# Moving one tile's load and its crossbar transfer ahead of a larger load, at the start of a fused attention and MLP kernel

## The chip, the cores and the metric

The kernel runs on one core of a Trainium2 chip. The metric is the time of one execution on the device, in microseconds (us). Each experiment is compared with the kernel before in interleaved rounds on one chip.

## The reference, cut to what matters

The input `x` has 2048 rows (tokens) of 640 numbers in bf16. One branch is a linear attention with 32 heads, the other a shift mixer with an MLP; a sigmoid gate mixes the two.

```python
qkv = x @ wqkv                       # -> q, k, v, 32 heads of 20
pq, pk = phi(q), phi(k)              # phi(t) = (t + 1 if t > 0 else exp(t)) + 1e-6
kv  = einsum("bhsd,bhse->bhde", pk, v)
o   = einsum("bhqd,bhde->bhqe", pq, kv) / den
a   = o.reshape(B, S, D) @ wo
# [...] b = MLP branch of x;  g = sigmoid(sum(x * gate_w))
return g * a + (1 - g) * b
```

This is about the first 20 us: `x @ wq` and `x @ wk` for the first tiles of 128 tokens each (tiles 0, 1, 2, ...).

## The kernel before

In this kernel TensorE (PE) reads `x` transposed (`xT`, features on the partitions) in both products. Tiles 0, 1 and 2 are transposed by PE itself. From tile 3 on, the SP queue issues a DMA for each tile that transposes `x_tok` (tokens on the partitions) into `xT` (`DMA_TRANSPOSE` in the traces); I call it a crossbar transfer. I call the transfer of tile t "Tt" (T3, T4, ...), and the load of tiles 4 to 7, one DMA of 640 KB, "XC1".

This is the order in which SP issues things in the kernel before:

```python
dma_in(x_tok[:, 0, :], x2[0:128, :], "x0")
dma_in(x_tok[:, 1, :], x2[128:256, :], "x1")
load_wq(0)
dma_in(x_tok[:, 2, :], x2[256:384, :], "x2")
for k in range(1, KD):                      # KD = 5 slices of the query weights
    load_wq(k)
for k in range(KD):                         # 5 slices of the key weights
    dma_in(wkg[:, k, 0:D], A_wqkv[128 * k:128 * (k + 1), D:2 * D], "wk%d" % k)
    if k == 2:
        dma_in(x_tok[:, 3, :], x2[384:512, :], "x3")
# [...]
for c in range(1, NCH):                     # c = 1 is XC1
    dma_in(x_tok[:, 4 * c:4 * c + 4, :], x2[512 * c:512 * (c + 1), :].rearrange("(n p) d -> p n d", p=128), "xc%d" % c)
    for t in range(3 if c == 1 else 4 * c, 4 * c + 4):
        sch.dma("sp", xT[:, :, 128 * t:128 * (t + 1)], x_tok[:, t, :], "trx%d" % (t % 4), transpose=True)
```

SP issues in this order in the traces. A transfer first waits for the load of its tile, and everything behind it on SP waits with it: tile 3's load landed at 9.84 us and T3 was issued at 9.85, XC1 landed at 13.52 and T4 was issued at 13.54, and SP issued nothing else while it waited. PE keeps the program's order too (first products of tiles 3, 4, 5 and 6 at 14.81, 17.53, 21.07 and 24.06 us). It goes through the first tiles like this:

```python
addA(("warm",), 0.0, lambda: warmup(WARM, 0.834))   # products on constants while the loads come
# [...] transposes of tiles 0, 1
addA(("q", 2), 4.08, q_three)                       # q of tiles 0, 1, 2 as the slices land
addA(("k", 1), 2.72, k_two)                         # k of tiles 0, 1
addA(("k", 2), 1.36, lambda: k_tile(2))
for i in range(3, NT + 2):
    # [...]
    addA(("q", i), 1.36, lambda t=i: q_tile(t))     # first use of tile i's xT: waits for Ti
    addA(("k", i), 1.36, lambda t=i: k_tile(t))
    # [...]
```

## Time and profile before

| | before |
|---|---|
| time, first 3 executions | 260.52 us median (260.36 to 261.09) |
| span of the profiled execution | 259.8 us |
| PE busy | 254.8 us (98%) |
| XC1: issued, landed | 7.41, 13.52 us |
| T3: issued, landed; PE starts on tile 3 | 9.85, 14.27; 14.75 us |
| T4: issued, landed; PE starts on tile 4 | 13.54, 17.45; 17.50 us |

"PE starts" is here, and in what follows, the first weight load of the tile's products.

Three lines of the page: the busy time of each engine, then the chain of work that ended last, by engine and by line of the kernel.

```profile
...
PE 254.8 (98%) x1655; PEld 133.0 (51%) x1686; DVE 152.0 (59%) x288; ACT 106.5 (41%) x216; POOL 93.6 (36%) x152
...
PE 98%; issue 1%; DVE 0%; POOL 0%; POOLq 0%
PE ps L600 61%; PE ps L1160 21%; PE ps L790 8%; PE ps L882 2%; PE ps L855 1%; PE ps L1072 1%; PE ps L1142 1%; PE ps L883 1%; PE ps L611 1%; DVE x_tok L639 0%; PE ps L962 0%; PE ps L991 0%; PE ps L1139 0%; POOL xn L659 0%; POOLq L1306 0%
...
```

PE is busy 98% of the span and makes up 98% of the chain: at each step back from the last instruction, what the work had waited for was other work of PE. (Some matmul records are missing from this trace: 1655 of 1686 are there. So the busy times of two traces are not to be subtracted.)

The list of PE's waits over the whole execution (line, what was waited for, us in total, times, longest):

```profile
...
PE ps L855 <- POOL xn L659: 1.1, 1, 1.1
PE ps L600 <- issue: 0.2, 1, 0.2
PE ps L1160 <- issue: 0.2, 1, 0.2
```

The only wait over 0.2 us is the one at the start.

The SP queue, from about 4 to 24 us (start, length, line; L285 is a plain load, L281 a crossbar transfer). The five transfers of 9.85 are merged into one line; between them SP waits for XC1.

```profile
...
4.08 0.43 SPq L285 DMA_DIRECT2D wq<-in_A_wqkv_dram  x1
4.56 1.38 SPq L285 DMA_DIRECT2D wkg<-in_A_wqkv_dram  x3
5.98 0.43 SPq L285 DMA_DIRECT2D x_tok<-in_A_x_dram  x1
6.46 0.91 SPq L285 DMA_DIRECT2D wkg<-in_A_wqkv_dram  x2
7.41 0.43 SPq L285 DMA_DIRECT2D x_tok<-in_A_x_dram  x1
9.85 9.57 SPq L281 DMA_TRANSPOSE xT<-x_tok  x5
19.47 0.58 SPq L285 DMA_DIRECT2D x_tok<-in_A_x_dram  x1
23.88 1.21 SPq L281 DMA_TRANSPOSE xT<-x_tok  x1
```

The issue of T4, and how long it takes to land; then PE's weight loads, whose times show when PE goes from one tile to the next (`wkg` is a key product of tile 3, the `wq` after it the first product of tile 4):

```profile
...
L281 SPq DMA_TRANSPOSE xT<-x_tok x1: 1207/1207/1207, 13.5 to 13.5; - x1
...
DMA to landing us min/median/max: 3.9/3.9/3.9
```

```profile
...
16.11 1.40 PEld L600 LDWEIGHTS ps<-wkg,xT 128*128 128x128 bf16 x10
17.50 1.38 PEld L600 LDWEIGHTS ps<-wq,xT 128*128 128x128 bf16 x10
```

T4 is issued at 13.54 and takes 3.92 us, so it lands at 17.45, and PE starts on tile 4 at 17.50. There is no idle time in brackets on that line. PE came to tile 4 just when the tile came.

### The profile page before, as it was taken

The numbers are of one execution on the slowest core, as the hardware profiler recorded it, in microseconds if no ns is written. First come the engines' busy times: TensorE is split into PE (matmuls) and PEld (weight loads), VectorE is DVE, ScalarE is ACT, GpSimd is POOL, SyncE is SP. The second block draws the span as 40 slices with busy tenths as digits, with TensorE's granted clock in tenths as the row PEclk, the third lists the DMA queues.
The fourth block names the chain that finished last, engine by engine and source line by source line (L and its number), as shares of the span: only waits on it lengthen the run. The fifth ranks groups of instructions, "written<-read, shape, count | busy, mean of one in ns | idle before, by whom it ended". The sixth has DMA issues, their size and how long they took to land.

```text
span 259.8 us, 4263 instructions
## 1 busy us (share of the span) xinstructions
PE 254.8 (98%) x1655; PEld 133.0 (51%) x1686; DVE 152.0 (59%) x288; ACT 106.5 (41%) x216; POOL 93.6 (36%) x152
## 2 busy tenths in 40 slices
PE   8999999999999999999999999999999999999996
PEld 4555555554445455555444545554455544455453
DVE  1487787899912799999998407993033410143233
ACT  1396767751355766685854140005500045200000
POOL 4003996869963019667904202230011110021001
DMA  6955886581756991552726650132000020000211
GB/s 185 288 86 150 175 207 154 166 140 39 110 113 124 360 327 32 76 101 52 104 46 122 124 73 0 39 83 82 0 3 0 3 101 0 0 3 1 103 50 50
DMA packets 51390, 25.16 MB, mean 97 GB/s; under 512 B 42750, under 2 KB 49959, under 8 KB 51370
## 3 DMA queue, kind: packets, MB, share of 16 engines
q1 hardware_dynamic: 49984, 21.47, 36.0%
q0 software_dynamic: 1136, 3.28, 5.1%
q8 instruction: 13, 0.21, 0.4%
q10 hardware_dynamic: 250, 0.14, 0.2%
q14 instruction: 7, 0.06, 0.1%
HBM read 12.05 MB, written 2.62 MB: 56 GB/s over the span
## 4 chain that ended last, share of the span: by engine, by line
PE 98%; issue 1%; DVE 0%; POOL 0%; POOLq 0%
PE ps L600 61%; PE ps L1160 21%; PE ps L790 8%; PE ps L882 2%; PE ps L855 1%; PE ps L1072 1%; PE ps L1142 1%; PE ps L883 1%; PE ps L611 1%; DVE x_tok L639 0%; PE ps L962 0%; PE ps L991 0%; PE ps L1139 0%; POOL xn L659 0%; POOLq L1306 0%
## 5 line engine op out<-in xcount | busy, mean ns | idle before, releaser
L600 PE MATMUL ps<-xnT,w 128*128 128x512 bf16 x348 | 80.4, 379 | 0.7 <-issue 0.2
L1160 PE MATMUL ps<-w,h2T 128*128 128x512 bf16 (+1 forms) x409 | 58.3, 298 | 0.5 <-issue 0.2
L656 ACT ACTIVATE h2T<-ps 128x512 bf16<-128x512 f32 x52 | 30.5, 598 | 67.6 <-PE ps L600 67.5
L600 PEld LDWEIGHTS ps<-xnT,w 128*128 128x128 bf16 x360 | 34.2, 98 | 38.5 <-issue 0.9
L639 DVE SCALAR_TENSOR_TENSOR x_tok<-ps,stg,abx 128x512 bf16<-128x512 f32 (+1 forms) x32 | 17.3, 550 | 61.5 <-PE ps L1160 61.5
L622 POOL TENSOR_SCALAR abx<-x_tok,stg 128x640 f32<-128x640 bf16 x16 | 15.3, 956 | 99.1 <-DVE x_tok L639 94.9
L1160 PEld LDWEIGHTS ps<-w,h2T 128*128 128x128 bf16 x416 | 32.1, 98 | 24.9 <-issue 1.1
L622 POOL TENSOR_SCALAR xn<-x_tok,st 128x640 bf16<-128x640 bf16 x32 | 34.9, 1099 | 13.8 <-DMA xnT<-xn 13.3
L656 ACT ACTIVATE Er<-ps 128x640 bf16<-128x640 f32 x32 | 22.4, 708 | 17.7 <-PE ps L600 7.9
L655 ACT ACTIVATE junk<-x_tok 128x640 bf16<-128x640 bf16 x32 | 23.7, 739 | 3.1 <-DVE x_tok L637 2.6
L656 ACT ACTIVATE hsT<-ps 128x512 bf16<-128x512 f32 (+1 forms) x32 | 18.9, 593 | 13.1 <-PE ps L600 12.7
L600 PE MATMUL ps<-M_sb,pqnT 128*128 128x128 bf16 (+1 forms) x156 | 23.6, 297 | 0.3
L600 PE MATMUL ps<-w,hsT 128*128 128x512 bf16 (+1 forms) x160 | 23.7, 299 | 0.0
L639 DVE SCALAR_TENSOR_TENSOR abx<-ps,stg,abx 128x640 f32<-128x640 f32 x16 | 14.1, 883 | 12.6 <-PE ps L600 11.6
L600 PE MATMUL ps<-wkg,xT 128*128 128x130 bf16 (+1 forms) x138 | 21.1, 298 | 0.1
L600 PE MATMUL ps<-wq,xT 128*128 128x128 bf16 (+1 forms) x128 | 19.7, 298 | 0.1
L600 PEld LDWEIGHTS ps<-w,hsT 128*128 128x128 bf16 x160 | 13.3, 98 | 12.1
L600 PEld LDWEIGHTS ps<-M_sb,pqnT 128*128 128x128 bf16 x160 | 13.2, 98 | 10.8
L790 PE MATMUL ps<-pk_tok,x_tok 128*128 128x512 bf16 x79 | 17.7, 379 | 0.1
L622 DVE TENSOR_SCALAR Er<-Er 128x640 bf16<-128x640 bf16 x32 | 11.6, 361 | 9.6 <-ACT Er L656 9.3
L1101 DVE TENSOR_TENSOR pq_tok<-pq_tok,dnr 128x300 bf16<-128x300 bf16 (+1 forms) x48 | 16.8, 403 | 0.6
L637 DVE SCALAR_TENSOR_TENSOR x_tok<-ps,x_tok 128x640 bf16<-128x640 f32 x16 | 13.1, 820 | 6.5 <-PE ps L600 5.9
(79 smaller groups left out, 229.1 us busy)
## 6 DMA issues: line engine op xcount, KB each, us to landing
w<-in_B_w_dram SPq DMA_DIRECT2D x1, 2160.0 KB, 9.7
w<-in_B_w_dram SPq DMA_DIRECT2D x1, 2080.0 KB, 15.2
x_tok<-in_A_x_dram SPq DMA_DIRECT2D x3, 640.0 KB, 5.5
out_dram<-x_tok SPq DMA_DIRECT2D x3, 640.0 KB, 3.1
w<-in_B_w_dram POOLq DMA_DIRECT2D x8, 160.0 KB, 3.7
wq<-in_A_wqkv_dram SPq DMA_DIRECT2D x5, 160.0 KB, 3.2
wkg<-in_A_wqkv_dram SPq DMA_DIRECT2D x5, 160.0 KB, 3.9
wv<-in_A_wqkv_dram POOLq DMA_DIRECT2D x1, 800.0 KB, 5.5
```

Of the source, the lines that this page charges most:

```text
L600: ins = e.matmul(out_ap, l, r, start=(i == 0), stop=(i == n - 1))
L611: ins = e.transpose(o, s_, ident[:])
L622: return engf(lambda e: e.tensor_scalar(out_ap, in_ap, s1, s2, op0, op1), rd, [out_ap], cost=cost)
L637: return dve(lambda e: e.scalar_tensor_tensor(out_ap, in0, scalar, in1, op0, op1, accum_out=accum), rd, [out_ap, accum], cost=cost + 70.0)
L639: return dve(lambda e: e.scalar_tensor_tensor(out_ap, in0, scalar, in1, op0, op1), rd, [out_ap], cost=cost)
L655: return act(lambda e: e.activation(out_ap, in_ap, func, bias=bias, scale=scale, accum_out=accum), rd, wr, cost=cost)
L656: return act(lambda e: e.activation(out_ap, in_ap, func, bias=bias, scale=scale), rd, wr, cost=cost)
L790: ins = e.matmul(o, l, r, start=(t0 + q_ == 0), stop=(t0 + q_ == NT - 1))
L855: ins = e.matmul(ps[:, b, 0:n], xn[:, 0, 0:128], xn[:, 0, 0:128].unsqueeze(1).to_broadcast([128, n // 128, 128]), start=True, stop=True)
L882: e.matmul(ps[:, b, 0:512], l, w[:, k, 0:512], start=(k == 0), stop=(k == KD - 1))
L1101: dve(lambda e, o=o, i0=i0, i1=i1: e.tensor_tensor(o, i0, i1, ALU.mult), [i0, dnr[:, 1, sd, :]], [o], cost=cost)
L1160: ins = e.matmul(o, l, r, start=False, stop=(i == KFF - 1), skip_group_check=(n0 > 0))
```

## The change

The intent is to have tile 3 earlier: its load goes behind the first key slice, and its transfer no longer stands behind the issue of XC1.

```diff
     for k in range(KD):
         dma_in(wkg[:, k, 0:D], ...)
-        if k == 2:
+        if k == 0:
             dma_in(x_tok[:, 3, :], x2[384:512, :], "x3")
+
+    def x_turn(t):
+        sch.dma("sp", xT[:, :, 128 * t:128 * (t + 1)], x_tok[:, t, :], "trx%d" % (t % 4), transpose=True)
+
+    x_turn(3)
     # [...]
     for c in range(1, NCH):
         dma_in(x_tok[:, 4 * c:4 * c + 4, :], ...)
-        for t in range(3 if c == 1 else 4 * c, 4 * c + 4):
-            sch.dma("sp", xT[:, :, 128 * t:128 * (t + 1)], x_tok[:, t, :], "trx%d" % (t % 4), transpose=True)
+        for t in range(4 * c, 4 * c + 4):
+            x_turn(t)
```

The instructions of PE, DVE, ACT and POOL and their waits are the same in both kernels; only the order on SP differs. (The line numbers of PE's groups behind the edit are 5 higher in the changed kernel.)

## The prediction

> **What bounds the kernel now.** TensorE. The page gives PE 254.8 of 259.8 us busy (98%), the chain of waits is 98% PE, and in the list of waits PE's only wait over 0.2 us is the 1.1 us at its start. Almost nothing is left to win: the change helps only where PE waits for a moved transfer, and hurts where it makes one late.
>
> **What the change does.** PE, DVE, ACT and POOL keep their order and waits; only the SP queue changes. Nothing is added or removed.
> 1. The load of x tile 3 moves from behind the third key slice to behind the first. Slices 1 and 2 move back one place.
> 2. Transfer T3 (crossbar transpose of tile 3) goes ahead of the load of tiles 4-7 (XC1). SP issues in order, so XC1 now waits behind T3's wait for tile 3 and T3's issue.
>
> **Costs, from the trace of before** (issues in the timeline, landings in the semaphore records). 128x640 loads land about 0.45 us apart (8.53, 8.97, 9.42, 9.84 for slices 0, 1, 2 and tile 3). XC1 was issued at 7.41 and landed at 13.5 (6.1 us). T3 was issued at 9.87 (SP held 1.3 us) and landed at 14.3. PE first uses tile 3 at 14.81, tile 4 at 17.50, tile 5 at 21.07, tile 6 at 24.06.
>
> After:
> - Tile 3 lands at about 8.97, slices 1 and 2 at 9.42 and 9.84; PE wants those at 10.97 and 11.25. No wait.
> - T3 is issued at about 9.0 and lands at 11.5 to 12.5. PE wants it at 14.81: 2 us earlier buys nothing.
> - XC1 is issued at about 10.3, 2.9 us later. Without T3 inside its stream it should take what the load of tiles 8-11 takes, also issued right behind a transfer: 4.4 us. It lands at about 14.7, 1.2 us later.
> - T4 waits for XC1. In before it was issued at 13.5; its last semaphore came at 17.46 and PE began on tile 4 at 17.50: no slack. [...] After, T4 is issued at about 14.75, where T5 was in before, and T5 landed at 17.95. So T4 lands at about 18.0, and PE waits about 0.5 us before tile 4.
> - T5-T7 and the loads of tiles 8-15 are about 1.2 us later: T5 at 19.3 against 21.07, T7 at about 22 against 27.05, T8 at about 27.5 against 30.04. No wait.
>
> **On the critical path:** a loss of about 0.5 us, once, and no gain. PE has no later idle time to absorb it.
>
> **Predicted time:** 261.0 us, 260.3 to 262.0 in 8 of 10. Faster by over 2%: 0.01; within 2%: 0.97; slower by over 2%: 0.02.
>
> **What would show it.** SP timeline: T3 at about 9.0, XC1 at about 10.3, T4 at about 14.7. T3 lands over 2 us before PE uses it. A new PE gap of 0.2 to 1 us before the first product of tile 4 at about 17.5, and none elsewhere. Everything later shifted by as much.
>
> **What would make it wrong.** If XC1, free of T3's interleaved packets, takes 3.5 us, T4 lands by 17.4 and nothing changes. If the stall of copies right behind a transfer (the load of tiles 8-11 lost about 1 us of its 4.4 so) is longer here[...], T4 lands after 18.5 and the loss is over 1 us. The spread of before's three runs is 0.7 us, so 0.5 us is near what they resolve.

An issue at about 14.75 and the 3.16 us that T5 took in before put T4's landing at about 18.0, 0.5 us after 17.50. The stall that the last paragraph names is in the trace of before: T7 landed at 20.66 us, and the load of tiles 8 to 11, issued at 19.47, moved at about 61 GB/s from 20.5 to 21.0 us and 49 from 21.0 to 21.5, against 394 from 22.0 to 22.5.

## The result, and the profile after

| | before | after |
|---|---|---|
| time, 6 executions each (the first 3 of before are those above) | 260.88 us median (260.36 to 261.12) | 260.93 us median (260.71 to 261.25) |
| ratio | | 1.0006, 95% interval 0.9992 to 1.0019 |
| XC1: issued, took, landed | 7.41, 6.11, 13.52 | 10.06, 4.38, 14.44 |
| T3: issued, took, landed | 9.85, 4.41, 14.27 | 8.71, 2.87, 11.58 |
| PE starts on tile 3 | 14.75 | 14.35 |
| T4: issued, took, landed | 13.54, 3.92, 17.45 | 14.45, 2.96, 17.41 |
| PE starts on tile 4 | 17.50 | 17.46 |

A ratio is the mean time of one kernel's fast executions over that of the other's of the same rounds, so it is not quite the ratio of the medians quoted beside it.

There is no difference that these executions resolve. But the chain has moved. The same three lines of the page:

```profile
...
PE 256.4 (99%) x1686; PEld 132.8 (51%) x1686; DVE 152.5 (59%) x288; ACT 106.6 (41%) x216; POOL 94.2 (36%) x152
...
PE 92%; DMA 4%; SPq 2%; DVE 0%; issue 0%
PE ps L600 60%; PE ps L1165 22%; PE ps L795 8%; DMA x_tok<-in_A_x_dram 3%; SPq L285 1%; DMA xT<-x_tok 1%; PE ps L1077 1%; PE ps L1147 1%; SPq L281 0%; DVE x_tok L639 0%; PE ps L967 0%; PE ps L996 0%; PE ps L1144 0%
...
```

PE's share of the chain fell from 98% to 92%, and the loads and transfers of `x` have come in with 4% and SP's issues with 2%. The list of PE's waits says the same: it has one that was not there before.

```profile
...
PE ps L860 <- POOL xn L659: 1.1, 1, 1.1
PE ps L600 <- DMA xT<-x_tok: 0.2, 1, 0.2
```

The SP queue, as above. T3 now stands alone at 8.71 and XC1 behind it at 10.06:

```profile
...
4.07 0.44 SPq L285 DMA_DIRECT2D wq<-in_A_wqkv_dram  x1
4.56 0.43 SPq L285 DMA_DIRECT2D wkg<-in_A_wqkv_dram  x1
5.03 0.43 SPq L285 DMA_DIRECT2D x_tok<-in_A_x_dram  x1
5.51 1.85 SPq L285 DMA_DIRECT2D wkg<-in_A_wqkv_dram  x4
8.71 1.30 SPq L281 DMA_TRANSPOSE xT<-x_tok  x1
10.06 0.57 SPq L285 DMA_DIRECT2D x_tok<-in_A_x_dram  x1
14.45 5.77 SPq L281 DMA_TRANSPOSE xT<-x_tok  x4
20.26 0.58 SPq L285 DMA_DIRECT2D x_tok<-in_A_x_dram  x1
```

T4, and PE's weight loads around the start of tile 4 (the first of the two lines is cut by the window; the brackets give the idle time of the weight loader and what ended it):

```profile
...
L281 SPq DMA_TRANSPOSE xT<-x_tok x1: 1806/1806/1806, 14.5 to 14.5; - x1
...
DMA to landing us min/median/max: 3.0/3.0/3.0
```

```profile
...
15.98 1.13 PEld L600 LDWEIGHTS ps<-wkg,xT 128*128 128x128 bf16 x8
17.46 1.36 PEld L600 LDWEIGHTS ps<-wq,xT 128*128 128x128 bf16 x10 [0.34 <-DMA xT<-x_tok]
...
```

And the part of the chain of waits from 5 to 20 us, in order of time (start, us, what). In before the same stretch of the chain is nothing but PE.

```profile
...
5.03 3.66 DMA x_tok<-in_A_x_dram
8.70 0.02 issue
8.71 1.30 SPq L281
10.01 0.05 issue
10.06 4.38 DMA x_tok<-in_A_x_dram
14.44 0.02 issue
14.45 2.96 DMA xT<-x_tok
17.41 0.05 issue
17.46 2.61 PE ps L600 x15
```

Read it downwards: tile 3's load, T3's issue, XC1, T4, and then PE on tile 4. This is the path that the prediction named. It was longer than PE's own work by about 0.34 us, the idle time of the weight loader, not by 0.5 us. (The 0.2 us in the list of waits is too small, because the ends of matmuls are modelled. From PE's start on tile 3 to its start on tile 5 it took 6.60 us here and 6.26 us in the first profile of before and in others without a wait: 0.34 us more.) And yet PE starts on tile 4 at the same time in the two profiles, 17.50 and 17.46. Two things have to be explained: why T4 did not land later than before, and why PE waited for it only in the changed kernel.

### The profile page after: what moved, and what is told of

It reads as the page before. It is cut to its first block, busy times and chain, and to the rows that moved or that the text cites. A ratio compares the mean times of both kernels' runs of the same rounds, so it can differ in the third digit from the quotient of the medians.

```text
span 259.7 us, 4294 instructions
## 1 busy us (share of the span) xinstructions
PE 256.4 (99%) x1686; PEld 132.8 (51%) x1686; DVE 152.5 (59%) x288; ACT 106.6 (41%) x216; POOL 94.2 (36%) x152
## 4 chain that ended last, share of the span: by engine, by line
PE 92%; DMA 4%; SPq 2%; DVE 0%; issue 0%
PE ps L600 60%; PE ps L1165 22%; PE ps L795 8%; DMA x_tok<-in_A_x_dram 3%; SPq L285 1%; DMA xT<-x_tok 1%; PE ps L1077 1%; PE ps L1147 1%; SPq L281 0%; DVE x_tok L639 0%; PE ps L967 0%; PE ps L996 0%; PE ps L1144 0%
## 5 line engine op out<-in xcount | busy, mean ns | idle before, releaser
L600 PE MATMUL ps<-xnT,w 128*128 128x512 bf16 x360 | 81.5, 379 | 0.0
L600 PE MATMUL ps<-M_sb,pqnT 128*128 128x512 bf16 (+1 forms) x160 | 24.3, 299 | 0.0
L600 PE MATMUL ps<-wq,xT 128*128 128x512 bf16 (+1 forms) x130 | 19.8, 299 | 0.2 <-DMA xT<-x_tok 0.2
L622 DVE TENSOR_SCALAR Er<-Er 128x640 bf16<-128x640 bf16 x32 | 11.6, 362 | 9.8 <-ACT Er L656 9.5
```

The source lines that it names most:

```text
L600: ins = e.matmul(out_ap, l, r, start=(i == 0), stop=(i == n - 1))
L622: return engf(lambda e: e.tensor_scalar(out_ap, in_ap, s1, s2, op0, op1), rd, [out_ap], cost=cost)
```

## The experiments

**Theory M.** What counts is when T3 and T4 land against the moment when PE comes to their tiles. The change gives T3 about 2.5 us of slack and takes some from T4. The size of the loss is small because (a) T4 of the first profile of before had been held up by something that has nothing to do with the order of the loads, and (b) the moment when PE comes to tile 4 moves from execution to execution with the turn of PE's clock.
**Rival B.** Where these transfers stand does not matter at all.
**Rival C.** The wait before tile 4 is made by the change, and before has none whenever the clock turns.

Landing times below are from the semaphore records of the trace: a DMA of this kernel has sixteen semaphore steps, and it has landed with the last one. "The clock turned" means the time at which PE's 128-column matmuls, 0.11 us apart at first, begin to come 0.055 us apart. The name is mine: the traces show this change of rate alone, and the granted clock of each of these profiled executions is listed as 1.0. Where PE stands still or runs 512-column products at that time, it is known to about 0.2 us only.

### The kernel before, twice more

No edit.

> The kernel before, run again unchanged. Theory M (masked): PE's start on tile 4 is held by the landing of T4 in before as well; it does not show there because PE's slow clock lasted to about 6.9 us in that profile and PE came to tile 4 just as T4 landed (17.46 against 17.50). So the result is 1.000 of before, T4 lands between 16.5 and 17.6, and whether PE waits before tile 4 depends on when its clock turned: turned by 6.3 us, a wait of 0.1 to 0.3 us as in after; turned at 6.9, none. Rival C (the change made the wait): no PE wait before tile 4 here whenever the clock turns.

Measured: 260.84 us median against 261.05 (ratio 0.9987, interval 0.9965 to 1.0008). T4 landed at 16.60, not at 17.46, 0.69 us before PE started on tile 4. The clock turned early, at about 5.3 us (6.9 in the first profile), so by theory M PE should have come early and waited for T4. It did not: it lost its lead at a key slice, for which it waited 0.4 us.

```profile
...
PE ps L882 <- DMA wkg<-in_A_wqkv_dram: 0.4, 1, 0.4
...
```

T3 had 0.14 us of slack.

> The kernel before a third time, for one more profile. Ratio 1.000 within 0.0015. T3 lands 3.5 to 6.5 us after its issue, T4 at 16.5 to 17.6. If T4's landing is what usually holds PE in before, a wait before tile 4 shows when its clock turned early and it did not lose that again to a weight slice; if T3 is, a wait before tile 3.

Measured: 261.08 us against 261.05 (ratio 1.0000, interval 0.9980 to 1.0021). Clock turned at about 5.1 us; PE lost its lead to a query slice (0.3 us) and a key slice (0.4 us). T3 landed at 14.83 and PE started on tile 3 0.04 us later; its matmuls of that tile came about 0.02 us late. T4 had 0.60 us of slack. So in three profiles of before PE's matmuls never waited for T4 (in the first, the weight loader may have, by 0.02 us). The part of theory M that expected T4 to hold before back as well is not borne out; rival C stands so far. What is borne out is that T4's landing at 17.46 in the first profile was not its usual one.

### The changed kernel again

No edit.

> The changed kernel again, unchanged. Theory M: T3 lands 2 us or more before PE uses it, XC1 takes 4.2 to 4.6 us, T4 is issued at 14.3 to 15.0 and lands at 16.9 to 17.6, PE waits 0 to 0.5 us before tile 4, the more the earlier its clock turned; T12 has under 2.5 us of slack (4 in before). Time 0.999 to 1.002 of before.

Measured: 260.69 us against 260.81 (ratio 0.9999, interval 0.9987 to 1.0011), so a second null result. XC1 was issued at 10.34 and took 4.11 us. T4 was issued at 14.46, within 0.01 us of the first profile, but landed at 16.92, and PE started on tile 4 at 17.08 with no wait. The clock turned at about the same time as in the first profile of the changed kernel (6.1 and 6.0 us), and in both PE was ready for tile 4 at 17.1 us. So the wait before tile 4 comes and goes within the changed kernel, with T4's 2.96 or 2.46 us; this falls against rival C in its strict form. T12 had 0.48 us of slack in the first profile and 0.81 in this one, against 4.12 and 3.78 in the first two of before.

### One half of the change at a time

Only the load of tile 3 moves; T3 stays behind XC1.

```diff
-        if k == 2:
+        if k == 0:
             dma_in(x_tok[:, 3, :], x2[384:512, :], "x3")
```

> Only the load of tile 3 moves; T3 stays behind the load of tiles 4-7 (XC1). XC1 is issued at 7.41 as in before. Theory M: T3 is issued at about 8.9, XC1 lands at about 13.0 to 13.5, T4 is issued then and its packets run before or beside the instruction fetch near 15.0 to 15.4. If the fetch alone made T4's straggler in before, T4 lands near 16 to 17.4 here; either way no PE wait over 0.1 us. Time 0.998 to 1.001 of before. Rival B (the place of XC1 does not matter at all): 1.000.

Measured: 260.81 us against 261.05 (ratio 0.9992, interval 0.9970 to 1.0015). T3 was issued at 8.63, 1.2 us sooner than in before, and landed at 14.89, 0.6 us later: it took 6.26 us (4.41 in before). XC1 took 6.72 us and landed at 14.13, later than expected. T3's packets ran all along beside those of XC1, and both suffered. PE had to wait before tile 3 (weight loader, 12 to 19 us):

```profile
...
PEld ps L600 <- DMA xT<-x_tok: 0.2, 1, 0.2
```

The expectation said no wait over 0.1 us, so that is a miss: here the earlier issue went with a later landing. (The "instruction fetch" of the expectation is the packet that the first profile lists as "instruction", at 15.36 to 16.35 us; that it delayed T4 there was a guess, from the times alone.)

Only T3 moves ahead of XC1; the load of tile 3 stays behind the third key slice.

```diff
         if k == 2:
             dma_in(x_tok[:, 3, :], x2[384:512, :], "x3")
+    x_turn(3)
     # [...]
-        for t in range(3 if c == 1 else 4 * c, 4 * c + 4):
+        for t in range(4 * c, 4 * c + 4):
```

> Only T3 moves ahead of XC1; the load of tile 3 stays behind slice 2. Theory M: T3 is issued at about 9.9, XC1 at 11.2, lands at 15.6, T4 is issued at 15.6 and lands at 18.4 to 18.8; PE waits 1.0 to 1.4 us before tile 4; time +0.8 to +1.3 us, ratio 1.003 to 1.005. Rival B: no change, 1.000 plus or minus 0.0015, and no PE wait that shows in the end time.

Measured: 262.05 us against 261.05 (ratio 1.0033, interval 1.0005 to 1.0061; one execution of 265.95 us, with a granted clock of 0.994, is left out of the ratio). XC1 was issued at 11.30 and landed at 15.56; T4 took 2.43 us and landed at 18.01. PE's wait before tile 4 is 1.3 us (1.43 us for the weight loader, below):

```profile
...
18.05 0.98 PEld L600 LDWEIGHTS ps<-wq,xT 128*128 128x128 bf16 x6 [1.43 <-DMA xT<-x_tok]
```

From PE's start on tile 3 to that on tile 5 it lost the 1.43 us. Rival B falls. The two halves belong together: T3 ahead of XC1 costs about 0.9 us (0.33% of 261) unless the load of tile 3 is early.

### More of the same delay

The changed kernel with one more crossbar transfer between T3 and XC1.

```diff
     x_turn(3)
+    sch.dma("sp", xnT[:, :, 0:128], x_tok[:, 3, :], "trxd", transpose=True)
```

> The changed kernel with one more crossbar transfer of tile 3, into a buffer that is written again later, between T3 and XC1 (a dose of delay). Theory M: XC1 is issued at about 11.4 (1.3 us after that of the changed kernel), lands at 15.8, T4 lands at about 18.7, PE waits 1.2 to 1.6 us before tile 4, and the whole is passed to the end: +1.0 to +1.5 us, ratio 1.004 to 1.006. Rival B (the place of XC1 does not matter): 1.000 plus or minus 0.0015.

Measured: 261.75 us against 261.05 (ratio 1.0036, interval 1.0007 to 1.0065). XC1 was issued at 11.71 and T4 landed at 18.35; PE waited 1.1 us before tile 4 (1.30 for the weight loader). The loss of most executions is about 0.7 us, a little under the expected 1.0 to 1.5. The profiled execution was the slowest of the six (263.62 us) and shows a second wait, which nobody had expected, before tile 13:

```profile
...
47.58 0.98 PEld L600 LDWEIGHTS ps<-wq,xT 128*128 128x128 bf16 x6 [1.87 <-DMA xT<-x_tok]
```

Its transfer T13 took 8.76 us (3.72 in the first profile of before), for which its later issue, by 2.8 us, and the loads of weights beside it are my guess, not tested (the packets of the weights' queue, q0, took 52.0% of the 16 engines' time from 36 to 46 us here, 44.0% from 34 to 44 us in before); 1.5 us of it passed between its fifteenth and its last semaphore step. This is the same erosion as T12's in the changed kernel, further on.

### What slows XC1: no T3 beside it

The kernel before without T3; tile 3 is transposed by PE.

```diff
-        for t in range(3 if c == 1 else 4 * c, 4 * c + 4):
+        for t in range(4 * c, 4 * c + 4):
     # [...]
+        if i == 3:
+            addA(("tx", 3), 0.28, lambda: t_x(3))
```

> The kernel before without T3: tile 3 is transposed by PE like tiles 0 to 2 (5 more transposes, about 0.3 us of PE), so that the load of tiles 4-7 (XC1) runs with no crossbar transfer beside it, issued at 7.41 as in before. If T3's packets are what made XC1 slow in before (6.1 and 6.3 us in two profiles, 6.7 where only the load moved), XC1 takes 4.8 to 5.6 us here and lands at 12.2 to 13.0; if it is only the key slices ahead of it in the queue, it takes 6 us or more again. T4 then lands by 16.2 with over 1 us of slack. Time 0.9995 to 1.0015 of before: the waits saved are paid with the transposes.

Measured: 265.06 us against 260.81 (ratio 1.0180). The time is a clear miss, for a reason beside the point: the copy of tile 3 out of PSUM stood on DVE behind other work, and PE waited 3.0 us for it. (Three of the six executions also show a lower granted clock, 0.987 to 0.994; the three at full clock took 264.17 to 264.48 us.) The quantity that the run was for came as expected. XC1, issued at 7.41 as in before, took 5.45 us; the profile rounds it up:

```profile
...
DMA to landing us min/median/max: 5.5/5.5/5.5
```

The three profiles of before have 6.11, 6.27 and 6.64 us, and the load-only kernel 6.72. So T3's packets cost XC1 0.7 to 1.3 us, by one profile of this kernel. T4 was expected by 16.2 us and landed at 17.23.

The late T4 is a straggler, as in the first profile of before: the last of its semaphore steps came long after the others. Among the transfers of the first 20 us, the last of a transfer's sixteen steps came over 1 us after the fifteenth in four traces, each time about 1.1 us after the end of a 16 KB packet on a queue that the page lists as "instruction":

| profile | transfer | 15th step | instruction packet | last step |
|---|---|---|---|---|
| before, first | T4 | 15.94 | 15.36 to 16.35 | 17.45 |
| no T3 (above) | T4 | 15.41 | 14.73 to 16.04 | 17.23 |
| keys first (below) | T4 | 16.89 | 16.31 to 17.32 | 18.41 |
| split only, again (below) | T5 | 15.58 | 15.01 to 16.03 | 17.13 |

In the other two profiles of before the packet was over by 15.03 and 15.30, ahead of most of T4's data, and T4 took 2.90 us in both with all sixteen steps within 0.2 us.

But a step can be as late without such a packet. In four profiles (before second and third, load only, split only) the last step of a key slice's load came 1.1 to 1.6 us after the fifteenth, at 11.6 to 12.6 us, and in no profile does an instruction packet run between 1 and 14 us. What delayed those is open.

### Taking away T4's wait for XC1

The changed kernel with the load of tile 4 taken out of XC1 and put ahead of T3.

```diff
+    dma_in(x_tok[:, 4, :], x2[512:640, :], "x4")
     x_turn(3)
     # [...]
     for c in range(1, NCH):
+        t0 = 5 if c == 1 else 4 * c
-        dma_in(x_tok[:, 4 * c:4 * c + 4, :], x2[512 * c:512 * (c + 1), :]...)
+        dma_in(x_tok[:, t0:4 * c + 4, :], x2[128 * t0:512 * (c + 1), :]...)
```

> The changed kernel with the load of tile 4 taken out of the load of tiles 4-7 and put ahead of T3; T4 then waits for tile 4 alone. Theory M: T3 lands by 12.5, T4 is issued at about 10.7 and lands by 15.5, tiles 5-7 land by 15 and T5 by 17.8 against about 20.9; PE waits before no tile of x from 3 on. What is left of PE's waits at the start are the loads of the weights. So the kernel is faster than the changed one by its wait before tile 4: 0.1 to 0.4 us, ratio to before 0.998 to 1.000. Rival B (where these transfers stand does not matter): equal to the changed kernel within 0.1 us.

Measured: 260.42 us against 260.81 of before (ratio 0.9987, interval 0.9975 to 0.9999), where the changed kernel had 260.69 (0.9999). T3 landed at 11.80 with 2.35 us of slack, T4 at 15.40 with 1.47, and T12 has 4.00 us of slack again. All of PE's waits:

```profile
...
PE ps L862 <- POOL xn L659: 1.1, 1, 1.1
PE ps L889 <- DVE xT L665: 0.4, 1, 0.4
```

> e4_split again, beside the others of this call: 260.4 to 260.7 us, ratio 0.998 to 0.9995; no wait of PE for a tile of x from 3 on.

Measured: 260.89 us against 261.21 (ratio 0.9979, interval 0.9963 to 0.9995): a time above the expected range, with before's too, and a ratio just below it. No wait for a tile of `x` from 3 on; the clock turned at 6.6 us in this profile and at 4.6 in the other. This version beats the kernel before, by 0.1 to 0.2%.

### The split without the change

The kernel before with only the load of tile 4 taken out of XC1. T3 stays behind all loads and beside their packets.

```diff
+        t0 = 5 if c == 1 else 4 * c
+        if c == 1:
+            dma_in(x_tok[:, 4, :], x2[512:640, :], "x4")
-        dma_in(x_tok[:, 4 * c:4 * c + 4, :], x2[512 * c:512 * (c + 1), :]...)
+        dma_in(x_tok[:, t0:4 * c + 4, :], x2[128 * t0:512 * (c + 1), :]...)
```

> The kernel before with only the load of tile 4 taken out of that of tiles 4-7; T3 stays behind the loads and beside their packets. This takes away the wait for T4 alone. If in the kernel before the landing of T3 holds PE back in those runs in which PE's clock turns early (so that the change does gain something by T3, and loses it again by T4), this kernel is about as before: T3 lands at 14.2 to 14.9, T4 by 16.5, ratio 0.999 to 1.001, and 0.2 to 0.4 us slower than e4. If T3 never holds PE in before, it is as fast as e4_split: ratio 0.998 to 0.999.

Measured: 260.38 us against 261.21 (ratio 0.9986, interval 0.9953 to 1.0019). Four of six executions took 260.19 to 260.40 us, but the profiled one took 263.27. In it T3 took 6.76 us, landed at 16.97, and PE waited for it:

```profile
...
PE ps L600 <- DMA xT<-x_tok: 1.7, 1, 1.7
...
```

> e6_split_only again. In its first run the profiled execution had T3 beside the loads for 6.8 us and PE waited 1.7 us for it (263.27 us), while four of the other five executions took 260.2 to 260.4 us. If T3 beside the packets of loads is unsteady, T3 takes anything from 3.5 to 7 us here, and some executions of the six are 0.5 us or more above their median; the median is 0.3 us or more under that of before, because T4 no longer waits for tiles 5-7.

Measured: 260.76 us (260.29 to 261.05) against 261.05 (ratio 0.9987, interval 0.9968 to 1.0007). T3 took 4.10 us and had 0.62 us of slack; no outlier this time. Both medians are below before's, as with the other split, but neither interval excludes 1. I had expected this kernel to be slower than the other split by 0.2 to 0.4 us if T3 usually holds before back. It is not. So T3 beside the loads does not usually hold PE; it does so now and then, and then by up to 1.7 us.

### All key slices ahead of tile 3

The split on the changed kernel, with the load of tile 3 behind the last key slice.

```diff
-        if k == 0:
+        if k == KD - 1:
             dma_in(x_tok[:, 3, :], x2[384:512, :], "x3")
```

> e4_split with the load of tile 3 behind the last key slice, so that slices 1 to 4 land one place earlier each. In two profiles PE waited 0.4 to 0.5 us for a key slice. If those waits still cost e4 something, this is faster than e4 by 0.05 to 0.2 us; T3 is issued at about 10.8 and lands at about 13.3 to 13.8, T4 lands at 16 to 17 and may become the wait. Otherwise equal to e4 within 0.1 us.

Measured: 262.18 us against 261.21 (ratio 1.0038, interval 1.0017 to 1.0058). T4 took 5.70 us, with the straggler of the table, and PE waited 0.8 us before tile 4. All six executions were slow for this family (261.55 us and up). Whether each had the straggler is not known: without it T4 would have been in by 16.9 us in the profiled one, before PE came at about 17.4. The early load of tile 3 is worth having; the key slices need no help at its expense.

### All landings side by side

| profile | clock turned | T3 took | T3's slack | T4 issued | T4 landed | weight loader's wait before tile 4 |
|---|---|---|---|---|---|---|
| before | 6.9 | 4.41 | 0.49 | 13.54 | 17.45 | none |
| before, second | 5.3 | 3.54 | 0.14 | 13.70 | 16.60 | none |
| before, third | 5.1 | 4.41 | 0.04 | 14.06 | 16.95 | none |
| changed | 6.0 | 2.87 | 2.78 | 14.45 | 17.41 | 0.34 |
| changed, second | 6.1 | 2.52 | 2.85 | 14.46 | 16.92 | none |
| load only | 4.1 | 6.26 | 0.04 | 14.15 | 16.96 | none |
| transfer only | 4.3 | 2.46 | 1.44 | 15.58 | 18.01 | 1.43 |
| one more transfer | 4.0 | 2.47 | 2.81 | 15.95 | 18.35 | 1.30 |

A slack of 0.04 is what is left where PE starts as soon as the tile is there.

## Why the prediction was right or wrong

The time was right: 261.0 us predicted, 260.93 measured, well inside the range. Of its steps:

- **PE bounds the kernel and nearly nothing is to be won.** Right. The ratio is 1.0006, and even the best kernel is only 0.1 to 0.2% faster.
- **The new order on SP.** Right to within 0.3 us: T3 issued at 8.71 (9.0 predicted), XC1 at 10.06 (10.3), T4 at 14.45 (14.75).
- **XC1 takes 4.4 us without T3 inside its stream.** Right: 4.38 and 4.11 us. The no-T3 run shows that T3's packets are one reason for the 6.1 us of before. An XC1 issued 2.65 us later therefore landed only 0.92 us later.
- **"PE waits about 0.5 us before tile 4."** The mechanism was right and the size was off. The chain of waits of the changed kernel is the predicted path, and delaying XC1 further costs 0.7 to 1.0 us by the medians. But the loss was 0.34 us in one profile and none in the other. Two terms of the sum were too large or too rigid. T4's landing was put at 18.0, from an issue at 14.75 and T5's 3.16 us; it was 14.45 with 2.96 us, and 14.46 with 2.46 us. And PE's arrival at tile 4 was taken as fixed at 17.50, from one profile in which the clock turned late; in the changed kernel's two profiles PE was ready at about 17.1 (17.46 less 0.34, and 17.08). An earlier arrival works towards a longer wait, so the two errors partly cancelled.
- **"no slack" of T4 in before.** Wrong as a general reading, right for that execution. 17.45 was a straggler. The other two profiles of before have T4 at 16.60 and 16.95, with 0.69 and 0.60 us of slack. What held the straggler's last step is not shown. Four traces here have the late step about 1.1 us after an instruction packet, but the records don't name the engine of a packet, so the link is by time alone, and the key slices had steps as late with no instruction packet near them.
- **"2 us earlier buys nothing"** for T3. Nearly true of the three profiles of before, but not a complete account. T3 had 0.49, 0.14 and 0.04 us of slack in before, and PE was held by about 0.02 us in the third. In the two other kernels with T3 behind the loads, it held PE 0.2 us (load only) and 1.7 us (split only). The change removes that exposure: T3's slack is 2.8 us. What the change gives is a steadier tile 3; what it takes is T4's margin, down from 0.6 us to 0.2 us or a short wait.
- **"No gain."** Doubtful, by the profiles, and the account of T3 and T4 alone leaves it out: the change also keeps the load of tiles 4 to 7 from standing right behind the key slices. In seven profiles that load (or that of tiles 5 to 7, behind tile 4's) is issued at 7.40 to 7.88 us (before three times, load only, no T3, split only twice). There the last slice landed at 10.95 to 12.56 us, and in four of them PE waited 0.4 to 0.7 us for a key slice. In the other seven it is issued at 10.06 us or later; there the last slice landed at 10.33 to 11.47 us and PE waited for no key slice. The two halves point the same way: last slice at 12.47 us and a wait of 0.5 us with the load only, 10.83 us and no wait with the transfer only. PE came to tile 3 at 14.35 us in both profiles of the changed kernel, but at 14.57 and 14.87 us in the second and third of before, although its clock had turned earlier there. A sooner PE meets T4 with less margin, so this is likely part of why PE waited for T4 in the changed kernel only. No run tests the gain in time by itself.
- **"No wait" for T8 to T15.** Right, but the size of the shift was underrated. I reckoned with 1.2 us; T12's slack fell from about 4 us to 0.5 and 0.8 us. In the first profile of the changed kernel T12 was issued 1.46 us later than in before (36.12 against 34.66) and took 5.31 us instead of 3.19; that the loads of weights beside it slow it is likely (their queue, q0, took 52.9% of the 16 engines' time while T12 ran, 10.1% in before), but was not tested.

What stays open: whether the small gains at the key slices and at T3 and the small loss at T4 cancel in an average execution, or all are nearly zero there. The profiles show these margins, but a profile is one execution, and executions of one kernel differ by more than any of them. Part of that spread may be PE's clock: it turned between about 4.0 and 6.9 us in the fourteen profiles, that is about 2.9 to 5.9 us after PE's first matmul at 1.05 us. What sets the turn, and what its spread costs in time, was not shown. How much of the split's 0.1 to 0.2% comes from T4's wait and how much from the key slices or the freer later transfers was not separated either.

## What to carry to other kernels

Moving a transfer ahead of a load on one queue delayed the load here by the transfer's wait and its issue (XC1 from 7.41 to 10.06 us, behind T3's issue at 8.71 and its 1.30 us on SP); ask what the next tile has left, before asking what this tile gains. A transfer that is issued earlier but behind a large load can land later (load only: issued 1.2 us sooner, landed 0.6 us later). When a tile is wanted first, load it by itself: the small separate load of tile 4 did what reordering the large one could not (T4 landed at 15.40 us with 1.47 us of slack, against 17.41 and 16.92 us in the changed kernel).

A transfer and a load side by side both took longer here. A 128x640 crossbar transfer took 2.45 to 2.51 us with no load beside it (T6 and T7 of before and of the changed kernel, first profiles) and 3.5 to 6.8 us beside loads (T3 of before and of the kernels that keep it behind the loads). The 640 KB load of tiles 4 to 7, issued right behind the key slices, took 5.45 us without and 6.1 to 6.7 us with such a transfer beside it.

One profile is one draw. A margin of 0.04 us in it, or the absence of a wait, may be a straggler or a late clock (T4 landed at 17.45 in the first profile of before and at 16.60 and 16.95 in the others; the clock turned at 6.9, 5.3 and 5.1 us); profile the kernel before two or three times before building a sum on it.
